# First group's inverse in blocks of sixteen joined by TensorE, single PSUM banks by name, and value transposes ahead of the state product

## The chip, the cores and the metric

One core of one Trainium2 chip runs the kernel. The metric is the device time of one execution in microseconds. Engines are TensorE (PE in the rows, with PEld for its weight loads), VectorE (DVE), ScalarE (ACT), GpSimd (POOL) and SyncE (SP), which issues most of the DMAs.

## The reference

A recurrent attention with a 40 x 40 state per head runs over 768 steps for 4 x 8 heads. Its output goes through a mixture of eight experts with a capacity, and then through a dense layer pair. Only the first part is touched by the change:

```
for t in range(S):
    y[:, :, t] = einsum('bhd,bhde->bhe', rt, state)
    Sa = einsum('bhde,bhe->bhd', state, at)
    state = state * wt[:, :, None, :] - einsum('bhd,bhe->bhde', Sa, bt) + einsum('bhd,bhe->bhde', vt, kt)
x = moe(y); out = relu(x @ w_in)**2 @ w_out
```

## The kernel before

**Chunks.** The 768 steps are cut into 24 chunks of 32 (`C`, `NC`). Within a chunk the recurrence is a triangular system: for each of the 32 heads a 32 x 32 strictly triangular matrix has to be inverted. One chunk fills eight columns of `GM`, `TT` and so on for four partition groups of 32, which makes 32 heads. Four chunks are a group, and one inverse serves a group.

**The inverse.** `inv_start` transposes `GM` to `L` (L228) and makes a list of jobs: seven small ones that build blocks of eight, two stages that double eight to sixteen, and two stages that double sixteen to thirty-two. A job is a product into a buffer `pr` and a sum over its last axis. `inv_all` (products L311, sums L314) does the first group's 27 jobs in one go before chunk 0; later groups are done by `inv` (L279, L283), so many jobs at a time, at places set by the tables `EARLY`, `FIRST`, `PLAN` and `LAST`. `inv_end` transposes the result to `TT` (L318), from which `block_T` copies block diagonals `TB` (L327).

**One chunk.** `scan` and `scale` (L158 to L189) turn the loaded tile `e` and `wB` into scaled factors. `gram` (L203) multiplies them to `G`, and `gram_mask` takes the two halves of `G` out of PSUM: ScalarE writes `GM`, VectorE writes `N`. `nat_n`, `nat_a`, `nat_pc` and `nat_k` lay out transposed copies. `solve` (px, L399) multiplies with `TB`, and ScalarE copies px to `lu`. `u` (pu) gives the new values, which ScalarE copies to `vu`. `state` (ps, L432) updates the state, `state_decay` writes it to `ru`, and `state_t` (pn) transposes it. `vu_t` (pv) transposes the values, ScalarE copies them to `vut`, `scores` (pq, L485) multiplies, and `scores_mask` (L493) masks on VectorE into `rq`. `y` (py) makes the output, `gate_in` writes `xt`, and the gate follows: `xT` (gpt), `logits` (pl), `choose`, `count` (pc), `rank`. `warm` issues matmuls whose results nobody reads.

**Order.** The whole attention part is written under a manual schedule: each engine does its instructions in the order of the Python calls in `run`. Chunks 1 to 19 run through `chunk(c)`, with m = c % 4; chunks 0 and 20 to 22 through the loop below it, chunk 23 by hand at the end. The expert part follows.

**PSUM.** Eight banks. Six are three double tiles, which `big` hands out in turn to G, pa, pk, px, pu, ps, pn, pv and most of the warm matmuls; two are single, handed out by `small` in turn to pq, py, gpt, pl, pc and the rest. A tile that is taken again waits until the readers of the one before are done:

```
return self.ps2.tile([128, 2, 512], F32, tag=f"b{self.nb % 3}", name=nm)
return self.ps1.tile([128, 512], F32, tag=f"s{self.ns % 2}", name=nm)
```

An fp32 matmul shows as two records in the trace, so that 32 matmuls stand there as x64.

Of the kernel before, what the change touches and what calls it, by code (L numbers as in the profile page):

```python
# [35 lines left out]
class Attention:  # L36
# [8 lines left out]
    def __init__(self, tc, es, gate, zt, eb, E, VN, VR, R0, R1, x, ident):  # L45
# [44 lines left out]
        self.st, self.nb, self.ns = {}, 0, 0  # L90
# [115 lines left out]
    def gram_mask(self, c, last=False):  # L206
# [9 lines left out]
        if not last:  # L216
            self.nc.scalar.mul(gm, gv[:, :, :, 0], -1.0)
        V.tensor_tensor(nn, gv[:, :, :, 1], self.mN.unsqueeze(1).unsqueeze(1).to_broadcast(bc), ALU.mult)
        if last:
            self.nc.scalar.mul(gm, gv[:, :, :, 0], -1.0)  # L220
# [80 lines left out]
    def inv_all(self):  # L301

        gi, jobs, _, _ = self.iv
        V = self.nc.vector
# [10 lines left out]
        self.inv_end()  # L315

# [86 lines left out]

    def u(self, c):
        A, V, T = self.nc.scalar, self.nc.vector, self.nc.tensor
        lu, rU, vu = self.lu, self.ru[c % 2], self.vu[c % 2]
        pu = self.big(f"pu{c}")
        for q in range(8):
            o, qq = q // 2, q % 2
            for par in range(2):  # L410
                for pp in range(2):
                    g, p = 2 * qq + pp, 64 * pp + 32 * par
                    T.matmul(pu[p : p + 32, q // 4, 40 * (q % 4) : 40 * (q % 4) + 40],
                             lu[:, par, o, 32 * g : 32 * g + 32], rU[:, par, q, 1 - pp, 0:40], start=True, stop=True)
# [81 lines left out]
    def y(self, c):  # L496
# [4 lines left out]
        py = self.small(f"py{c}")  # L501
# [29 lines left out]
    def run(self, extra, weights):  # L531
        LA, SHIFT = 7, 20
        EARLY, FIRST, PLAN, LAST = 4, (11, 8, 6, 2), (7, 5, 3, 1), (6, 5, 5, 0)
# [23 lines left out]
        self.warm(W0, self.zt, 320, True)  # L557
        for c in range(4):
# [13 lines left out]
        self.scan(4)  # L572
        self.scale(4)
# [29 lines left out]
        def chunk(c):  # L603
# [11 lines left out]
            if not done:  # L615
# [3 lines left out]
                self.gram_mask(c + LA)  # L619
# [54 lines left out]
            if ahead:  # L674
# [4 lines left out]
                self.gram_mask(c + LA + 1, True)  # L679
# [14 lines left out]
        def warm0(i):  # L694
            if c == 0:
                self.warm(W2[i], self.zt, 320, True)

        for c in range(NC - 1):
# [14 lines left out]
            if c == 0:  # L713
                self.gram(5)
# [23 lines left out]
            if c == 0:  # L738
                warm0(2)
# [101 lines left out]
class Gate:  # L841
# [44 lines left out]
    def xT(self, c):  # L886
# [4 lines left out]
        pt = self.at.small(f"gpt{c}")  # L891
# [8 lines left out]
    def logits(self, c):  # L900
# [4 lines left out]
        pl = self.at.small(f"pl{c}")  # L905
# [35 lines left out]
    def count(self, c0, c1):  # L941
# [3 lines left out]
        pc = self.at.small(f"pc{c0}")  # L945
# [796 lines left out]
```

## Time and profile before

| | us |
|---|---|
| median of 3 runs | 1092.46 (1089.16 to 1092.53) |
| profiled execution | 1095.65 |
| its span | 1093.9 |
| first px (chunk 0) starts | 69.66 |
| px of chunk 1 starts | 90.86 |
| attention part ends, about | 472 |

The span is what the trace covers; the execution's own time is 1.75 us longer. Times in the rows count from the span's start. Chunks are told apart by their matmuls: u(c) starts at 154.76 for c = 4, 221.95 for c = 8, 289.15 for c = 12, 351.45 for c = 16 and 402.41 for c = 20.

### The profile page before, as it was taken

To read this page: it belongs to the slowest core of one execution; us is meant where nothing else is said; L and a number is where in the kernel's file an instruction comes from. 1 tells how busy PE (TensorE), PEld (TensorE's weight loads), DVE (VectorE), ACT (ScalarE), POOL (GpSimd) and SP (SyncE) were. 2 spreads that over 40 slices of the span, in tenths; PEclk is the share of its full clock that TensorE was granted. 3 is DMA by queue.
4 is the path that set the end of the run, shared out by engine and by line. 5 is a ranking of instruction groups with operands and counts; after the bars stand their busy time and mean duration, and the time that the engine had idled before them with its cause. 6 is when DMAs were issued, how large, how long until landed. Compare 5 with 4: busy or idle time off the path is not lost.

```text
span 1093.9 us, 30647 instructions
## 1 busy us (share of the span) xinstructions
PE 932.5 (85%) x12526; PEld 838.5 (77%) x12526; DVE 744.2 (68%) x1486; ACT 585.8 (54%) x1330; POOL 313.8 (29%) x443
## 2 busy tenths in 40 slices
PE   4337788778787878898989998899999999999995
PEld 2236677667676767778979998789889899999995
DVE  5889989797899774558878878957544444444432
ACT  8125666676767877435545555456444353434332
POOL 4533225253354301115545555314301010000000
PEclk7668877896989998899989999899999999999998
DMA  7645634635453333165676766523100000000000
GB/s 183 148 134 149 210 92 146 182 111 166 141 150 94 98 110 110 43 179 163 210 227 204 217 216 200 163 85 105 49 25 25 25 25 25 1 25 1 25 1 28
DMA packets 80647, 122.71 MB, mean 112 GB/s; under 512 B 9679, under 2 KB 57409, under 8 KB 79561
## 3 DMA queue, kind: packets, MB, share of 16 engines
q1 hardware_dynamic: 71173, 100.09, 31.0%
q10 hardware_dynamic: 7020, 12.78, 4.1%
q0 software_dynamic: 2304, 7.78, 2.2%
q8 instruction: 101, 1.65, 0.6%
q14 instruction: 49, 0.40, 0.1%
HBM read 91.36 MB, written 29.35 MB: 110 GB/s over the span
## 4 chain that ended last, share of the span: by engine, by line
PE 56%; DVE 20%; ACT 10%; issue 5%; DMA 4%; POOL 3%; SPq 1%; ACTq 0%; DVEq 0%; POOLq 0%
PE phg L1405 16%; PE pog L1431 5%; PE pog L1430 5%; PE pog L1429 5%; PE phe L1405 4%; PE px L399 4%; DVE pr L279 2%; DMA xs<-zs_s 2%; PE ps L432 2%; ACT TB L327 2%; PE pq L485 2%; DVE pr L311 1%; PE poe L1431 1%; PE poe L1429 1%; PE poe L1430 1%
## 5 line engine op out<-in xcount | busy, mean ns | idle before, releaser
L1415 DVE SCALAR_TENSOR_TENSOR sqg<-phg,rg 128x512 f32<-128x512 f32 x96 | 66.3, 691 | 119.0 <-ACT rg L1414 116.8
L1414 ACT ACTIVATE rg<-phg 128x512 f32<-128x512 f32 x96 | 57.2, 596 | 110.4 <-PE phg L1405 110.2
L1417 DVE TENSOR_TENSOR hlg<-sqg,hhg 128x512 fp32r<-128x512 f32 x96 | 66.6, 694 | 65.9 <-ACT hhg L1416 61.1
L1416 ACT CAST hhg<-sqg 128x512 fp32r<-128x512 f32 x96 | 59.6, 620 | 78.6 <-DVE sqg L1415 76.2
L399 PE MATMUL px<-TB,X 128*104 128x128 f32 x384 | 66.1, 344 | 33.9 <-ACT TB L327 33.7
L1405 PE MATMUL phg<-xhg,e 128*128 128x512 f32 x264 | 93.1, 393 | 0.0
L399 PEld LDWEIGHTS px<-TB,X 128*104 128x104 f32 x384 | 60.5, 226 | 36.5 <-ACT TB L327 34.9
L1431 PE MATMUL pog<-e,hlg 128*128 128x320 f32 x240 | 74.2, 309 | 0.0
L1430 PE MATMUL pog<-e,hhg 128*128 128x320 f32 x240 | 74.1, 309 | 0.0
L1429 PE MATMUL pog<-e,hhg 128*128 128x320 f32 x240 | 73.9, 308 | 0.0
L186 POOL TENSOR_TENSOR e<-e 104x512 f32<-104x512 f32 x21 | 27.5, 1309 | 149.2 <-DVE e L162 79.5
L186 POOL TENSOR_TENSOR e<-e,wB 104x512 f32<-104x512 f32 x42 | 56.2, 1356 | 33.4 <-DVE wB L158 30.3
L1223 POOL TENSOR_TENSOR e<-rw,e 128x256 fp32r<-128x256 f32 x51 | 43.2, 851 | 69.3 <-ACT e L1222 65.5
L1405 PE MATMUL phe<-xhe,e 128*128 128x480 f32 (+4 forms) x176 | 58.6, 373 | 0.0
L1405 PEld LDWEIGHTS phg<-xhg,e 128*128 128x128 f32 x264 | 49.6, 188 | 8.9
L1544 POOL DMA_INDIRECT x2g<-zs_s,idx x24 | 23.7, 989 | 113.5 <-ACT hhg L1416 105.7
L327 ACT COPY TB<-TT 32x256 f32<-32x256 f32 x94 | 37.8, 402 | 34.5 <-DVE TT L318 28.4
L485 PE MATMUL pq<-rq,vut 128*64 128x64 f32 x768 | 39.2, 246 | 18.4 <-ACT vut L476 16.8
L203 PE MATMUL G<-e 64*32 64x64 f32 (+1 forms) x1536 | 24.0, 248 | 36.2 <-POOL e L186 23.1
L1431 PE MATMUL poe<-e,hle 128*120 128x320 f32 (+4 forms) x150 | 47.3, 315 | 7.2 <-DVE hle L1410 7.2
L203 PEld LDWEIGHTS G<-e 40*32 40x32 f32 (+1 forms) x1536 | 18.7, 117 | 43.6 <-POOL e L186 30.8
L1405 PE MATMUL phg<-xlg,e 128*128 128x512 f32 x132 | 51.8, 392 | 0.0
(340 smaller groups left out, 2920.5 us busy)
## 6 DMA issues: line engine op xcount, KB each, us to landing
e<-in_E_dram ACTq DMA_DIRECT2D x60, 208.0 KB
rw<-in_w_dram SPq DMA_DIRECT2D x30, 320.0 KB
zs_s<-zt SPq DMA_DIRECT2D x24, 320.0 KB
rw<-in_w_dram SPq DMA_DIRECT2D x30, 256.0 KB
e<-in_E_dram SPq DMA_DIRECT2D x9, 832.0 KB
ru<-in_VR_dram SPq DMA_DIRECT2D x48, 128.0 KB
cr<-in_wi_dram SPq DMA_DIRECT2D x20, 256.0 KB
cr<-in_wo_dram SPq DMA_DIRECT2D x20, 256.0 KB
```

Of the source, the lines that this page charges most:

```text
L186: eng.tensor_tensor(z, z, f, ALU.mult)
L327: (copies[g] if copies else self.nc.scalar.copy)(self.TB[c % 2][t, :, t], self.TT[t, 8 * (c % 4) : 8 * (c % 4) + 8])
L399: self.nc.tensor.matmul(px[0:104, par, 128 * o : 128 * o + 128], X[:, par, o, :], TB[:, 4 * par + o, :], start=True, stop=True)
L485: T.matmul(pq[s, 64 * q : 64 * q + 64], vut[:, q, s], rt[:, :, q, pp], start=True, stop=True)
L1405: T.matmul(o, lt, rt, start=(i == 0), stop=(i == len(seq) - 1))
L1414: A.activation(r[:, :n], o, AF.Relu)
L1415: V.scalar_tensor_tensor(sq[:, :n], o, 0.0, r[:, :n], ALU.max, ALU.mult)
L1416: A.copy(hh[:, :n], sq[:, :n])
L1417: V.tensor_tensor(hl[:, :n], sq[:, :n], b32(hh)[:, :n], ALU.subtract)
L1429: T.matmul(o, hh[:, t], W["h2"], start=(f == 0), stop=False)
L1430: T.matmul(o, hh[:, t], W["l2"], start=False, stop=False)
L1431: T.matmul(o, hl[:, t], W["h2"], start=False, stop=(f == NF - 1))
```

## The change

Five things, all within the attention part.

1. `inv_all` becomes `inv_blocks`: the first group's inverse stops at blocks of sixteen. A second, half transpose makes `nat`, and `join(c)` fills the missing sixteen-wide block of a chunk by two sets of 32 small matmuls (jl and jr) with a ScalarE copy between them and four copies behind. `join(0)` stands before the first `block_T`, `join(1)` behind `solve(0)`, `join(2)` and `join(3)` in chunk 0.
2. In the first four chunks and in `ahead`, VectorE's half of `gram_mask` comes before ScalarE's. `scan(4)` and `scale(4)` stand ahead of the first inverse's start, `scan(5)` ahead of `join(0)`.
3. PSUM is two double tiles in turn (G, pa, pk, ps, pn) and four single banks by name: 0 for pu and jl, 1 for px's and pv's first half and pq, 2 for py, gpt, pl, jr and the counts' pc of the first batches, 3 for the second halves of px and pv, for warm and for the later pc.
4. In `chunk`, `vu_t` stands ahead of `state`, and `state_decay` right behind it, on VectorE where m is 0 instead of on ScalarE. `scores` does one half of the partitions first, then the other. `nat_a` stands ahead of the gate's `xT`.
5. `EARLY` goes from 4 to 1, and the tables give those three jobs back: `PLAN` (8, 5, 4, 2), `LAST` (8, 6, 5, 0).

```diff
     def big(self, nm):
         self.nb += 1
-        return self.ps2.tile([128, 2, 512], F32, tag=f"b{self.nb % 3}", name=nm)
-
-    def small(self, nm):
-        self.ns += 1
-        return self.ps1.tile([128, 512], F32, tag=f"s{self.ns % 2}", name=nm)
+        return self.ps2.tile([128, 2, 512], F32, tag=f"b{self.nb % 2}", name=nm)
+
+    def bank(self, k, nm):
+        return self.ps1.tile([128, 512], F32, tag=f"k{k}", name=nm)
...
-    def inv_all(self):
+    def inv_blocks(self):
 
         gi, jobs, _, _ = self.iv
+        jobs = [j for j in jobs if j[0] < 9]
...
         self.inv_end()
+        nat = self.p2.tile([128, 512], F32, tag="prod", name="nat", bufs=3)
+        self.nat = nat.rearrange("p (a s) -> p a s", s=16)
+        V.transpose(self.nat.rearrange("p a s -> p s a"), self.Tt[:, 0:16])
+
+    def join(self, c, copies=None):
+
+        A, T = self.nc.scalar, self.nc.tensor
+        blocks = range(8 * c, 8 * c + 8)
+        groups = [slice(32 * g, 32 * g + 32) for g in range(4)]
+        p1, p2 = self.bank(0, f"jl{c}"), self.bank(2, f"jr{c}")
+        m = self.p2.tile([128, 512], F32, tag="prod", name=f"jm{c}", bufs=3)[:, 0:128]
+        for k, a in enumerate(blocks):
+            for s in groups:
+                T.matmul(p1[s, 16 * k : 16 * k + 16], self.GM[s, a], self.TT[s, a, 16:32], start=True, stop=True)
+        A.copy(m, p1[:, 0:128])
+        for k, a in enumerate(blocks):
+            for s in groups:
+                T.matmul(p2[s.start : s.start + 16, 16 * k : 16 * k + 16], self.nat[s, a], m[s, 16 * k : 16 * k + 16],
+                         start=True, stop=True)
+        for g, s in enumerate(groups):
+            h = slice(s.start, s.start + 16)
+            (copies[g] if copies else A.copy)(self.TT[h, 8 * c : 8 * c + 8, 16:32],
+                                              p2[h, 0:128].rearrange("p (a t) -> p a t", t=16))
...
-        px = self.big(f"px{c}")
+        px = [self.bank((1, 3)[par], f"px{par}_{c}") for par in range(2)]
...
-        pu = self.big(f"pu{c}")
+        pu = self.bank(0, f"pu{c}")
...
-        pv = self.big(f"pv{c}")
...
+        pv = [self.bank((1, 3)[pp], f"pv{pp}_{c}") for pp in range(2)]
...
-        pq = self.small(f"pq{c}")
-        for q in range(8):
-            for pp in range(2):
+        pq = self.bank(1, f"pq{c}")
+        for pp in range(2):
+            for q in range(8):
...
-        EARLY, FIRST, PLAN, LAST = 4, (11, 8, 6, 2), (7, 5, 3, 1), (6, 5, 5, 0)
+        EARLY, FIRST, PLAN, LAST = 1, (11, 8, 6, 2), (8, 5, 4, 2), (8, 6, 5, 0)
...
-        self.gram_mask(3, True)
+        self.scan(4)
+        self.gram_mask(3)
+        self.scale(4)
         self.inv_start(0, lambda k, h: G if (h, k) in POOL else V)
...
-        self.inv_all()
+        self.inv_blocks()
         self.load(8)
         A = self.nc.scalar
-        self.block_T(0, (A.copy, V.tensor_copy, A.copy, V.tensor_copy))
+        split = (A.copy, V.tensor_copy, A.copy, V.tensor_copy)
         self.scan(5)
+        self.join(0, split)
+        self.block_T(0, split)
         self.scale(5, (V, G, V))
         self.load_w(8)
         self.warm(W3)
         self.solve(0)
+        self.join(1)
...
             fill(c, 0)
+            self.vu_t(c)
             self.state(c)
-            if c % 2:
-                self.state_decay(c)
+            self.state_decay(c, None if c % 2 else V.tensor_copy if done else self.nc.scalar.copy)
             self.load(c + LA + 2, 3)
-            self.vu_t(c)
-            if c % 2 == 0:
-                self.state_decay(c, self.nc.scalar.copy)
...
+            self.nat_a(c + 2)
+            self.nat_n(c + 2)
+            self.nat_pc(c + 2)
             gate.xT(c - 1)
...
-            self.nat_n(c + 2)
-            self.nat_a(c + 2)
-            self.nat_pc(c + 2)
...
             if c == 0:
+                self.join(2)
                 self.gram(5)
...
             if c == 0:
+                self.join(3)
                 warm0(2)
...
-        pc = self.at.small(f"pc{c0}")
+        pc = self.at.bank(2 if c0 < 14 else 3, f"pc{c0}")
```

TensorE's order from the last Gram product before chunk 0 to the first ones in it. Before:

```order
L203 MATMUL G_480<-e_139 32x64 x32
L399 MATMUL px_612<-TB_108,X_104 104x128 x8
L413 MATMUL pu_636<-ru_110,lu 32x40 x32
L355 MATMUL pk_673<-ident_59,e_129 128x104 x8
L529 MATMUL warm<-zt 128x320
L203 MATMUL G_690<-e_362 32x64 x32
L432 MATMUL ps_730<-vu_112,rhsY_118 40x40 x32
```

And in the changed kernel at the same place:

```order
L202 MATMUL G_480<-e_139 32x64 x32
L329 MATMUL jl_568<-TT,GM 32x16 x32
L333 MATMUL jr_569<-jm_570,nat 16x16 x32
L422 MATMUL px_0_650<-TB_108,X_104 104x128 x4
L422 MATMUL px_0_651<-TB_108,X_104 104x128 x4
L329 MATMUL jl_662<-TT,GM 32x16 x32
L333 MATMUL jr_663<-jm_664,nat 16x16 x32
L436 MATMUL pu_747<-ru_110,lu 32x40 x32
L378 MATMUL pk_784<-ident_59,e_129 128x104 x8
L550 MATMUL warm<-zt 128x320
L329 MATMUL jl_801<-TT,GM 32x16 x32
L333 MATMUL jr_802<-jm_803,nat 16x16 x32
```

Two joins now stand between the first px and the next Gram product, and pu comes behind one of them.

TensorE's order in chunk 1, from the state product on. Before:

```order
L432 MATMUL ps_1126<-vu_113,rhsY_119 40x40 x32
L473 MATMUL pv_1163<-ident_59,vu_113 80x64 x16
L485 MATMUL pq_1197<-rq_117,vut 64x64 x16
L894 MATMUL gpt_1226<-ident_59,xt_1187 128x128 x2
L894 MATMUL gpt_1226<-ident_59,xt_1187 64x128
L355 MATMUL pa_1235<-ident_59,e_137 128x104 x8
L459 MATMUL pn_1248<-ident_59,ru_110 128x40 x16
```

In the changed kernel, from the last two value transposes on:

```order
L494 MATMUL pv_1_1384<-ident_59,vu_113 80x64
L494 MATMUL pv_1_1385<-ident_59,vu_113 80x64
L454 MATMUL ps_1404<-vu_113,rhsY_119 40x40 x32
L506 MATMUL pq_1456<-rq_117,vut 64x64 x16
L378 MATMUL pa_1485<-ident_59,e_137 128x104 x8
L917 MATMUL gpt_1500<-ident_59,xt_1446 128x128 x2
L917 MATMUL gpt_1500<-ident_59,xt_1446 64x128
L481 MATMUL pn_1507<-ident_59,ru_110 128x40 x16
```

ps has moved between pv and pq, and pa ahead of gpt.

TensorE's order in chunk 20 from the scores on, with the semaphores that each waits for. Before:

```order
L485 MATMUL pq_7147<-rq_116,vut 64x64 [waits DMAHW3_49,DMAHW1_49,Activation_49]
L485 MATMUL pq_7147<-rq_116,vut 64x64 [waits Activation_49]
L485 MATMUL pq_7147<-rq_116,vut 64x64 x14
L399 MATMUL px_7166<-TB_109,X_105 104x128 [waits PE_49]
L399 MATMUL px_7166<-TB_109,X_105 104x128 x7
L948 MATMUL pc_7183<-oh,mats 128x16 [waits PE_49,Activation_49]
```

In the changed kernel:

```order
L506 MATMUL pq_7443<-rq_116,vut 64x64 [waits Activation_49]
L506 MATMUL pq_7443<-rq_116,vut 64x64 x7
L422 MATMUL px_21_7462<-TB_109,X_105 104x128 [waits DVE_49,PE_49]
L422 MATMUL px_21_7462<-TB_109,X_105 104x128 x3
L422 MATMUL px_21_7463<-TB_109,X_105 104x128 x4
L971 MATMUL pc_7480<-oh,mats 128x16 [waits Activation_49]
```

px has a wait for VectorE that it did not have; the wait of pc for ScalarE now stands behind px's second half on the same bank.

## Rows read from the trace of the kernel before

**Rows 1.** The page, part 1: busy us, share of the span, instructions.

```profile
PE 932.5 (85%) x12526; PEld 838.5 (77%) x12526; DVE 744.2 (68%) x1486; ACT 585.8 (54%) x1330; POOL 313.8 (29%) x443
```

**Rows 2.** Stretches: length, busy us of PE, PEld, DVE, ACT, POOL, clock, DMA.

```profile
154.76:221.95 67.19, 54.53 (x1526) 49.01 (x1525) 56.89 (x102) 45.09 (x107) 24.81 (x41) 0.80 0.47 141
...
289.15:351.45 62.30, 48.50 (x1524) 42.78 (x1524) 56.88 (x101) 45.25 (x107) 29.85 (x48) 0.95 0.44 128
...
402.40:451.00 48.60, 40.30 (x1093) 36.16 (x1085) 22.66 (x64) 34.50 (x87) 4.61 (x5) 0.86 0.32 96
```

**Rows 3.** Timeline up to the inverse: start, us, instruction, idle before and releaser.

```profile
8.47 0.18 DVE L168 TENSOR_TENSOR Pc<-wB,e 104x16 f32<-104x16 f32 x1 [3.31 <-DMA e<-in_E_dram]
...
13.89 1.23 DVE L162 TENSOR_TENSOR_SCAN e<-e,ones 104x512 f32<-104x512 f32 x1 [2.42 <-DMA e<-in_E_dram]
...
22.83 0.42 DVE L218 TENSOR_TENSOR N<-G,mN 128x256 f32<-128x256 f32 x1 [4.55 <-ACT GM L217]
...
40.56 0.14 DVE L311 TENSOR_TENSOR pr<-L,Tt 128x4 f32<-128x4 f32 x1
40.72 1.26 POOL L186 TENSOR_TENSOR e<-e 104x512 f32<-104x512 f32 x1 [6.85 <-DVE pr L311]
...
46.84 0.63 DVE L311 TENSOR_TENSOR pr<-L,Tt 128x256 f32<-128x256 f32 x2
```

**Rows 4.** Timeline at the end of the first inverse.

```profile
51.79 2.10 DVE L311 TENSOR_TENSOR pr<-L,Tt 128x512 f32<-128x512 f32 x2
...
66.75 2.01 DVE L318 STREAM_TRANSPOSE TT<-Tt 128x1024 f32<-128x1024 f32 x1
...
69.66 3.46 PE L399 MATMUL px<-TB,X 128*104 128x128 f32 x16 [24.02 <-ACT TB L327]
...
71.20 1.23 DVE L158 TENSOR_TENSOR_SCAN wB<-wB,seeds 104x512 f32<-104x512 f32 x1
```

**Rows 5.** Timeline of the second group's inverse, first and eighth product.

```profile
95.13 0.24 DVE L279 TENSOR_TENSOR pr<-L,Tt 128x4 f32<-128x4 f32 x1
...
99.06 0.43 DVE L279 TENSOR_TENSOR pr<-L,Tt 128x256 f32<-128x256 f32 x1
```

**Rows 6.** Timeline of TensorE in chunk 0, to the px of chunk 1.

```profile
75.06 0.80 PE L413 MATMUL pu<-ru,lu 128*32 128x40 f32 x64 [1.94 <-DVE N L218]
...
83.22 0.85 PE L203 MATMUL G<-e 64*32 64x64 f32 x64 [1.82 <-DVE e L186]
...
89.75 1.18 PE L203 MATMUL G<-e 64*32 64x64 f32 x64 [3.25 <-DVE Pc L168]
...
90.86 3.11 PE L399 MATMUL px<-TB,X 128*104 128x128 f32 x16
```

**Rows 7.** Timeline of chunk 5 (first row) and of chunk 12.

```profile
180.93 0.90 PE L894 MATMUL gpt<-ident,xt 128*128 128x128 f32 x3 [0.97 <-DVE xt L516]
...
292.26 1.43 PE L432 MATMUL ps<-vu,rhsY 128*40 128x40 f32 x64
...
292.91 0.59 ACT L402 COPY lu<-px 104x512 f32<-104x512 f32 x1
...
294.97 0.33 PE L485 MATMUL pq<-rq,vut 128*64 128x64 f32 x2 [0.70 <-ACT vut L476]
...
301.67 0.62 PE L910 MATMUL pl<-wg,gxT 128*32 128x8 f32 x24 [3.27 <-ACT rhsY L463]
```

**Rows 8.** Timeline of chunks 19 and 20.

```profile
400.05 1.38 DVE L493 TENSOR_TENSOR rq<-pq,mQ 64x512 f32<-64x512 f32 x2
...
402.41 0.80 PE L413 MATMUL pu<-ru,lu 128*32 128x40 f32 x64
...
412.17 2.89 PE L399 MATMUL px<-TB,X 128*104 128x128 f32 x16
412.29 1.39 DVE L493 TENSOR_TENSOR rq<-pq,mQ 64x512 f32<-64x512 f32 x2 [3.03 <-PE pq L485]
...
415.15 1.07 ACT L402 COPY lu<-px 104x512 f32<-104x512 f32 x2 [3.24 <-PE px L399]
```

More of the change, by code (lines that the diff above doesn't have):

```diff
@@ L204, in gram, with gram_mask @@
                              e[r, 512 + 64 * i : 576 + 64 * i], start=True, stop=True)
-    def gram_mask(self, c, last=False):
+    def gram_mask(self, c, first=True):
         if c >= NC:
@@ L215, in gram_mask @@
         bc = [128, 2, 4, 32]
-        if not last:
+        if not first:
             self.nc.scalar.mul(gm, gv[:, :, :, 0], -1.0)
         V.tensor_tensor(nn, gv[:, :, :, 1], self.mN.unsqueeze(1).unsqueeze(1).to_broadcast(bc), ALU.mult)
-        if last:
+        if first:
             self.nc.scalar.mul(gm, gv[:, :, :, 0], -1.0)
@@ L412, in u @@
                     g, p = 2 * qq + pp, 64 * pp + 32 * par
[L413 removed]
+                    T.matmul(pu[p : p + 32, 40 * q : 40 * q + 40],
                              lu[:, par, o, 32 * g : 32 * g + 32], rU[:, par, q, 1 - pp, 0:40], start=True, stop=True)
@@ L467, in vu_t @@
         vu = self.vu[c % 2]
-        pv = self.big(f"pv{c}")
-        for h in range(2):
-            for i in range(4):
-                for pp in range(2):
-                    s = slice(64 * pp, 64 * pp + 64)
-                    T.transpose(pv[0:80, pp, 256 * h + 64 * i : 256 * h + 64 * i + 64],
-                                vu[s, pp, 4 * h + i].rearrange("p r d -> p (r d)"), self.ident[s, s])
+        pv = [self.bank((1, 3)[pp], f"pv{pp}_{c}") for pp in range(2)]
+        for q in range(8):
+            for pp in range(2):
+                s = slice(64 * pp, 64 * pp + 64)
+                T.transpose(pv[pp][0:80, 64 * q : 64 * q + 64], vu[s, pp, q].rearrange("p r d -> p (r d)"),
+                            self.ident[s, s])
         for pp in range(2):
-            A.copy(self.vut[0:80, :, 64 * pp : 64 * pp + 64], pv[0:80, pp].rearrange("p (q z) -> p q z", q=8))
+            A.copy(self.vut[0:80, :, 64 * pp : 64 * pp + 64], pv[pp][0:80].rearrange("p (q z) -> p q z", q=8))
     def scores(self, c):
@@ L480, in scores @@
         rt, vut = self.RT(c), self.vut
-        pq = self.small(f"pq{c}")
-        for q in range(8):
-            for pp in range(2):
+        pq = self.bank(1, f"pq{c}")
+        for pp in range(2):
+            for q in range(8):
                 s = slice(64 * pp, 64 * pp + 64)
@@ L500, in y @@
         lY, rY, pn = self.lhsY(c), self.rhsY[c % 2], self.st.pop(("Pn", c))
-        py = self.small(f"py{c}")
+        py = self.bank(2, f"py{c}")
         for o in range(4):
@@ L522, in store_x, with warm @@
         self.nc.sync.dma_start(self.x.rearrange("(b c t) f -> c b t f", b=4, c=NC)[c], self.gate.xt[c])
-    def warm(self, n, r=None, cols=512, small=False):
-        w = self.small("warm").unsqueeze(1).to_broadcast([128, 2, 512]) if small else self.big("warm")
+    def warm(self, n, r=None, cols=512):
+        w = self.bank(3, "warm").unsqueeze(1).to_broadcast([128, 2, 512])
         r = self.Tt.rearrange("p a b -> p (a b)") if r is None else r
@@ L556, in run @@
         G.memset(self.Tt.rearrange("p a b -> p (a b)")[:, 0:1024:33], 1.0)
-        self.warm(W0, self.zt, 320, True)
+        self.warm(W0, self.zt, 320)
         for c in range(4):
@@ L571, in run @@
         self.load_r(0)
-        self.scan(4)
-        self.scale(4)
         gate.init()
@@ L695, in warm0 @@
             if c == 0:
-                self.warm(W2[i], self.zt, 320, True)
+                self.warm(W2[i], self.zt, 320)
         for c in range(NC - 1):
@@ L890, in xT @@
         xt = self.xt[c]
-        pt = self.at.small(f"gpt{c}")
+        pt = self.at.bank(2, f"gpt{c}")
         for k in range(3):
@@ L904, in logits @@
         xT = self.xTt.pop(c)
-        pl = self.at.small(f"pl{c}")
+        pl = self.at.bank(2, f"pl{c}")
         for k in range(3):
```

15 lines of the change are left out of this document (7 added, 8 removed).

## The prediction

> **What bounds the kernel now.** I read the page first, then the stretches, then the timeline of the places that the diff touches. TensorE is busy 85% of the span and VectorE 68% [rows 1], but that is a mean over stages. The diff ends with the attention part; the expert part after it keeps its instructions, so whatever the attention part gains or loses in its last microsecond is passed on whole. Within the attention part there are four stages. Up to the first px at 69.66 VectorE runs alone, and its inverse is the chain. In chunk 0, from px at 69.66 to px at 90.86, TensorE waits three times for what VectorE delivers [rows 4, 6]. In chunks 1 to 18 the two take turns: a stretch of four chunks takes 67.2 or 62.3 us with VectorE busy 56.9 in both [rows 2]. From chunk 19 VectorE has less to do and TensorE's order decides.
>
> **First stage.** Four steps move the first px.
> - VectorE's first N waits 4.55 us for ScalarE, which reads the same G [rows 3]. With the order turned, it can run at 18.28. Loads hold it next: VectorE got the first two E at 8.47 and 13.89, 5.4 apart, so the third is there at 19.3, the fourth at 24.7, the fifth with its wB near 30. Then a scan pair (two scans of 1.23 [rows 4] with the small steps between them, 3.0), N and GM (0.42 each, as N's row) and a transpose (2.0) lead to the first product at 36.5 instead of 40.56: -4.0. Bounds -1.5 (loads later) and -4.55.
> - The seven small products took 40.56 to 46.84, 6.28 us, beside GpSimd's multiplications of scale(4), which begin at 40.72 [rows 3]; the same seven took 3.93 in the second group [rows 5]. Scale(4), three pieces of 1.26, can now start at 33.4, before N and the transpose, and ends at 37.2, just after the first product begins: one slowed product is left. I take -1.5, bounds 0 and -2.35. [...]
> - The sixteen-wide stage, from 51.8 to the transpose at 66.75, goes: -14.9 [rows 4].
> - Between the transpose's end and px stood 0.9 us. Now nat's transpose (half of 2.01: 1.0), the scan pair of chunk 5 (3.0) and TT's copies on VectorE (0.55) stand there, with the join of TensorE and ScalarE beside them: 32 matmuls, a copy, 32 matmuls, a copy, 3.0 if 32 matmuls cost 1.2, as G's do [rows 6]. Net +4.4; bounds +3 and +6.
>
> The first px: 69.66 - 4.0 - 1.5 - 14.9 + 4.4 = 53.7, 16.0 earlier.
>
> **Chunk 0.** It held 21.2 us from px to px. Three more joins stand in TensorE's order, each 32 + 32 matmuls with a ScalarE copy between (0.3, half of lu's 0.59 for four times the columns [rows 7]): 2.7, together +8.1 (at 0.80 for 32, as pu's [rows 6], +5.7). ScalarE reaches the copies of joins 2 and 3 late, behind four TB copies and two ru copies: +3.8 (0 to 5). The px of chunk 1 now takes a bank that scores(0) filled, and its mask stands behind scan(8) in VectorE's order: +2.0. Against that the three waits fall away, 1.94, 1.82 and 3.25 [rows 6], since VectorE comes 16 us earlier: -7.0. Sum +6.9, so the next px comes at 81.7, not 90.86: **-9.2** of the 16.0 stay. Bounds -13 and -6.
>
> **Chunks 1 to 18**, for each four:
> - In the first of the four, pl waits 3.27 for a bank that the mask frees late [rows 7]; on its own bank it doesn't. Two products with sums fewer stand before the mask and the gate's input; at 1.05 for a product [rows 4] and 0.4 for a sum (a pass over 256 columns takes 0.43 [rows 5]) that is, with smaller shapes among them, some -2.4. VectorE takes ru's two copies from ScalarE there: +1.6 (a 64x512 pair is 1.39 [rows 8]). VectorE being the chain at this place, -0.8.
> - pa goes ahead of gpt, which waited 0.97 for VectorE [rows 7]: -0.9.
> - The transposes of the values stand ahead of the state product, so the 1.43 us of ps cover ScalarE's copy for which pq waited 0.70 [rows 7]. In two chunks of four I count all of it, in the third half (ps must wait for pk's copies, with two double buffers instead of three), in the first nothing: there pv takes px's banks and must wait until lu is copied, 293.50, where ps could start at 292.26 [rows 7]. -1.75.
> - One more product and sum stands between the last mask and the transpose: +1.45.
>
> That is -2.0 for four chunks, **-9.0** over 4.5. Bounds: 0 where VectorE eats it, and -21 where all stretches fall to VectorE's own 56.9 + 1.6 [rows 2].
>
> **Chunks 19 to 23.** Here the new banks cost. px lies on banks 1 and 3, pq on bank 1, the gate's counts on bank 3.
> - Chunk 19: px was done before the mask (400.05 to 401.43) began, and pu followed at 402.41 [rows 8]. Now px waits for the mask's end: 2.9 for px and 0.7 of the transposes behind it, +3.6.
> - Chunk 20: px started at 412.17 with the mask at 412.29; now after it, +1.5. The counts then wait for lu's copies, which end at 416.22 where px ended at 415.06 [rows 8]: +1.2. With a slower px, +3.3.
> - Chunk 21 +1.5 (mask alone); chunk 22 +2.6 (mask, and the warm matmul on bank 3 behind lu); chunk 23 +1.7 (counts behind vut's copies, two of the same size as lu's 1.07).
>
> Sum **+12.7**; behind these matmuls stand y, pa, pl and the next u, for which all wait. Bounds +7 (lu's first half copied while px's second half runs) and +18 (a lower clock on top). For the other terms, cost is nothing: nat on VectorE beside the join (1.0 if not), GM after N on an idle ScalarE.
>
> **Sum:** -9.2 - 9.0 + 12.7 = -5.5. The profiled execution took 1095.65 us (span 1093.9), 3.2 over the median of 1092.46; the difference is put on the median: 1087.0.
>
> **The rivals.**
> - *The start is kept*: joins 2 and 3 hide under VectorE and ScalarE comes in time, -13 instead of -9.2, and the tail costs its lower bound 7: -15, 1077.5. For it: TensorE idles 7.0 us in chunk 0 [rows 6]. Against: the join's copies stand in ScalarE's order behind others. 0.17.
> - *The clock rises in the middle*: the stretch from 154.76 had a granted clock of 0.80 and kept TensorE busy 54.5 us; that from 289.15 had 0.95 and 48.5 for as many instructions, and took 4.9 us less [rows 2]. If fewer waits bring two stretches there, -10 more: 1077. 0.10.
> - *The clock falls in the tail*: the waits added from chunk 19 leave TensorE idle, and its clock goes to the lower level more often. At the price that separates the two stretches, 6.0 of busy time, the tail is +18.7: 1093, no change. 0.08. [...]
> - *VectorE eats the middle*: two fewer early products come back as the late one, no gain in chunks 1 to 18: +3.5, 1096. For it: VectorE is 85 to 91% busy there. 0.17.
> - *Slower*: pv, moved ahead of ps, stalls on lu's copies not in one chunk of four but in every chunk that solves ahead. Place: between px and pv; price 1.24 [rows 7] in the ten others, +12.4: 1099. It decides from 0.9 us per chunk on, where the gain of 5.5 has become a loss of 3.3. Against: in the others y, pk and G stand between. 0.12.
>
> **How the numbers follow.** The forecast has 0.36 and its own range 1082 to 1092. The range takes in 1077 and leaves out the slower rival and what lies beyond the bounds: 1075 to 1098. About 0.3%, 3.3 us, is what a measurement here can tell from no change, so faster is below 1089.2. Faster: 0.28 of the forecast, 0.17, 0.10 and 0.02 make 0.57. Slower: 0.12, and 0.10 of the middle eaten, 0.22. The rest, 0.21, is no change.
>
> **What would show it.** First px near 53.7, the second near 81.7; no N waiting for ScalarE before the first inverse. Scores starting without a wait for vut in chunks 1 to 18, ps directly ahead of them. In chunks 19 to 22 px beginning at the mask's end, and pc or warm behind lu. I am wrong if px(0) is earlier by 16 and px(1) by as much, if the stretches of four shrink by over 5 us, or if the last chunks take no longer than the 48.6 us that they did from 402.40 to 451 [rows 2].

## The result, and the profile after

The changed kernel takes 1104.5 us (four executions, 1103.2 to 1107.4), the kernel before 1092.5 beside it: 1.0113 times as long, interval 1.0076 to 1.0151. Six more executions gave 1103.9 (1.0122, 1.0078 to 1.0166). The forecast was 1087.0 and its range ended at 1098, so it is wrong in sign and outside the range. The kernel before scatters by itself: 35 executions lay between 1081.3 and 1103.2, with a median of 1091.7.

The table shows where the time went, in the profiled execution of each kernel (1107.4 and 1095.65 us). u(c) is the start of pu of chunk c on TensorE, and pte is the first matmul of the expert part:

| | before | after | difference |
|---|---|---|---|
| first px | 69.66 | 54.05 | -15.6 |
| px of chunk 1 | 90.86 | 83.35 | -7.5 |
| u(1) | 94.71 | 85.96 | -8.7 |
| u(8) | 221.95 | 211.00 | -11.0 |
| u(16) | 351.45 | 341.56 | -9.9 |
| u(19) | 388.06 | 375.32 | -12.7 |
| u(20) | 402.41 | 397.88 | -4.5 |
| u(21) | 417.80 | 419.44 | +1.6 |
| u(22) | 433.22 | 434.85 | +1.6 |
| u(23) | 450.39 | 455.02 | +4.6 |
| first pte of the expert part | 469.11 | 475.80 | +6.7 |
| end of the span | 1093.9 | 1105.7 | +11.8 |

Up to chunk 19 the kernel is ahead by 12.7 us. Chunks 19 to 23 lose 19.4, and the expert part another 5.1, which a second profile below shows to be scatter. The page's first part says nothing of this; VectorE has even less to do than in [rows 1]:

```profile
PE 952.9 (86%) x13038; PEld 857.6 (78%) x13038; DVE 733.2 (66%) x1477; ACT 586.3 (53%) x1340; POOL 305.3 (28%) x439
```

The stretches are four chunks, u(12) to u(16), and then chunks 19 to 23 whole (from u(19) to the first pte). Columns as in [rows 2]: length, busy us of PE, PEld, DVE, ACT, POOL, granted clock, DMA share, GB/s.

```profile
277.26:341.56 64.30, 53.36 (x1525) 47.37 (x1524) 59.97 (x106) 44.43 (x106) 31.05 (x48) 0.87 0.43 124
375.32:475.80 100.48, 73.14 (x1614) 63.82 (x1607) 48.68 (x165) 50.01 (x127) 10.96 (x12) 0.81 0.25 73
```

The four chunks from 277.26 took 64.30, with VectorE busy for 59.97 of it; the same four took 62.30 in [rows 2]. Chunks 19 to 23 took 100.48 us for TensorE's 73.14 busy ones. The same chunks in the kernel before:

```profile
388.06:469.11 81.05, 67.64 (x1622) 58.99 (x1615) 47.23 (x166) 48.90 (x127) 10.74 (x12) 0.86 0.30 88
```

So of the 19.4 lost, 5.5 are slower matmuls (about as many of them, at a granted clock of 0.81 instead of 0.86) and 13.9 are idle time. A second profile of the changed kernel has 102.3 us for the same chunks.

VectorE's timeline (start, duration, idle before and its releaser in brackets) shows that the first stage went as planned:

```profile
17.91 0.41 DVE L217 TENSOR_TENSOR N<-G,mN 128x256 f32<-128x256 f32 x1
...
36.83 0.92 DVE L311 TENSOR_TENSOR pr<-L,Tt 128x4 f32<-128x4 f32 x1
...
41.43 1.15 DVE L311 TENSOR_TENSOR pr<-L,Tt 128x256 f32<-128x256 f32 x2
...
46.42 2.01 DVE L341 STREAM_TRANSPOSE TT<-Tt 128x1024 f32<-128x1024 f32 x1
48.24 1.08 DVE L318 STREAM_TRANSPOSE nat<-Tt 128x512 f32<-128x512 f32 x1
```

N at 17.91 no longer waits for ScalarE, where it waited 4.55 [rows 3]; the first product is at 36.83 (36.5 was forecast), and the seven small ones are done at 41.43, after 4.60 instead of 6.28. No sixteen-wide stage follows; the transpose does at 46.42. TensorE in chunk 0:

```profile
54.05 3.71 PE L422 MATMUL px<-TB,X 128*104 128x128 f32 x16 [3.41 <-DVE TB L350]
...
66.45 0.72 PE L333 MATMUL jr<-jm,nat 32*16 32x16 f32 x64 [2.37 <-ACT jm L330]
...
74.31 0.69 PE L333 MATMUL jr<-jm,nat 32*16 32x16 f32 x64 [2.05 <-ACT jm L330]
...
83.35 1.97 PE L422 MATMUL px<-TB,X 128*104 128x128 f32 x16 [0.75 <-DVE rq L514]
```

Joins 2 and 3 wait 2.37 and 2.05 for ScalarE's copy, and the second px 0.75 for the mask.

TensorE from 90 to 374 us, which is all but the ends of chunks 1 to 18, grouped by line: busy us and mean ns, then the idle time ahead of the group and what ended it.

```profile
L506 PE MATMUL pq<-rq,vut 128*64 128x64 f32 x576 | 36.2, 229 | 4.8 <-issue 4.1 <-ACT vut L497 0.7
L454 PE MATMUL ps<-vu,rhsY 128*40 128x40 f32 x1152 | 28.0, 216 | 2.2 <-ACT rhsY L411 2.2
...
L378 PE MATMUL pa<-ident,e 104*128 104x104 f32 x144 | 16.8, 260 | 6.3 <-DVE N L217 6.3
...
L528 PE MATMUL py<-rhsY,rq 128*32 128x40 f32 x1152 | 16.3, 218 | 4.5 <-ACT lg L934 4.5
...
L494 PE MATMUL pv<-ident,vu 64*80 64x64 f32 x288 | 13.4, 230 | 2.7 <-ACT lu L425 2.7
...
L917 PE MATMUL gpt<-ident,xt 128*128 128x128 f32 (+1 forms) x54 | 10.2, 302 | 5.7 <-DVE xt L537 5.7
L933 PE MATMUL pl<-wg,gxT 128*32 128x8 f32 (+1 forms) x408 | 8.8, 188 | 10.6 <-ACT gxT L920 10.6
```

Before, over its own chunks 1 to 18 (94.71 to 388.06), pq idled 16.8 us, 15.8 of it for vut:

```profile
L485 PE MATMUL pq<-rq,vut 128*64 128x64 f32 x576 | 30.2, 244 | 16.8 <-ACT vut L476 15.8 <-issue 1.1
```

There pl idled 8.0, py 0.9, ps 0.7, pa nothing, and pv did not wait for lu. In the changed kernel the wait for vut is down to 0.7, as meant. In its place pl waits 10.6 for gxT, pa 6.3 for N, py 4.5 for lg, pv 2.7 for lu, ps 2.2.

TensorE in chunks 19 and 20:

```profile
380.57 1.90 PE L506 MATMUL pq<-rq,vut 128*64 128x64 f32 x32 [0.34 <-ACT vut L497]
390.53 3.71 PE L422 MATMUL px<-TB,X 128*104 128x128 f32 x16 [8.06 <-DVE rq L514]
394.03 1.59 PE L378 MATMUL pa<-ident,e 104*128 104x104 f32 x8
395.42 0.71 PE L917 MATMUL gpt<-ident,xt 128*128 128x128 f32 x3
396.06 0.69 PE L481 MATMUL pn<-ident,ru 40*128 40x40 f32 x16
397.46 0.49 PE L933 MATMUL pl<-wg,gxT 128*32 128x8 f32 x24 [0.72 <-ACT gxT L920]
397.88 0.80 PE L436 MATMUL pu<-ru,lu 128*32 128x40 f32 x64
...
409.92 3.42 PE L422 MATMUL px<-TB,X 128*104 128x128 f32 x16 [1.58 <-DVE rq L514]
414.07 1.06 PE L971 MATMUL pc<-oh,mats 128*128 128x16 f32 x8 [0.73 <-ACT lu L425]
...
419.02 0.49 PE L933 MATMUL pl<-wg,gxT 128*32 128x8 f32 x24 [2.29 <-DVE xt L537]
```

and ScalarE and VectorE at the first of these waits:

```profile
383.29 1.64 ACT L350 COPY TB<-TT 32x256 f32<-32x256 f32 x4 [2.29 <-DVE ab L980]
...
386.90 1.66 DVE L469 TENSOR_TENSOR ru<-ps,Pc 40x640 f32<-40x640 f32 x2
...
389.00 1.38 DVE L514 TENSOR_TENSOR rq<-pq,mQ 64x512 f32<-64x512 f32 x2
```

px of chunk 20 idles 8.06 us until the mask is done, although TB, its last input, was there at 384.93. The scores that the mask reads had ended at 382.47, but VectorE did the gate's ranks, ru and xt first and came to the mask at 389.00. px then takes 3.71 us, where the same px took 1.99 before,

```profile
396.33 1.99 PE L399 MATMUL px<-TB,X 128*104 128x128 f32 x16 [0.52 <-ACT TB L327]
```

and all that follows (pa, gpt, pn, pl) stands behind it: from the mask's end at 390.38 to pu at 397.88 are 7.5 us, where [rows 8] had 1.0.

### The profile page after: what moved, and what is told of

Its sections match the earlier page's. It is cut to its first block, busy times and chain, and to the rows that moved or that the text cites. A ratio compares the mean times of both kernels' runs of the same rounds, so it can differ in the third digit from the quotient of the medians.

```text
span 1105.7 us, 31651 instructions
## 1 busy us (share of the span) xinstructions
PE 952.9 (86%) x13038; PEld 857.6 (78%) x13038; DVE 733.2 (66%) x1477; ACT 586.3 (53%) x1340; POOL 305.3 (28%) x439
## 4 chain that ended last, share of the span: by engine, by line
PE 54%; DVE 23%; DMA 8%; ACT 7%; issue 5%; SPq 1%; POOL 1%; ACTq 0%; DVEq 0%; POOLq 0%
PE phg L1428 16%; PE pog L1454 5%; PE pog L1453 5%; PE pog L1452 5%; DVE pr L278 5%; PE phe L1428 4%; PE px L422 3%; PE pq L506 2%; DMA xs<-zs_s 2%; DVE rq L514 2%; DVE Tt L282 2%; DMA wB<-in_E_dram 2%; DVE e L161 1%; DMA rw<-in_w_dram 1%; PE ps L454 1%
## 5 line engine op out<-in xcount | busy, mean ns | idle before, releaser
L185 POOL TENSOR_TENSOR e<-e,wB 104x512 f32<-104x512 f32 x42 | 55.4, 1335 | 35.1 <-DVE wB L157 26.4
L506 PE MATMUL pq<-rq,vut 128*64 128x64 f32 x768 | 52.6, 242 | 5.7 <-issue 4.1
L506 PEld LDWEIGHTS pq<-rq,vut 128*64 128x64 f32 x768 | 49.1, 154 | 7.7 <-issue 5.4
L1432 ACT ACTIVATE hhe<-phe 128x480 fp32r<-128x480 f32 (+4 forms) x64 | 33.9, 529 | 33.2 <-PE phe L1428 33.0
L514 DVE TENSOR_TENSOR rq<-pq,mQ 64x512 f32<-64x512 f32 x48 | 32.9, 685 | 21.9 <-PE pq L506 21.2
```

Source lines behind the costliest of these rows:

```text
L185: eng.tensor_tensor(z, z, f, ALU.mult)
L506: T.matmul(pq[s, 64 * q : 64 * q + 64], vut[:, q, s], rt[:, :, q, pp], start=True, stop=True)
```

## Experiments

For chunks 19 to 23 there are three theories. A: the shared single banks lengthen them. B: the moved orders make VectorE or ScalarE late. C: TensorE's clock is lower. For the middle: either the new banks take back what the moves earn, or VectorE is the chain and nothing done to TensorE's waits counts. Times are medians of 6 to 12 executions of the experiment and 17 to 35 of the kernel before beside them.

**Scores off px's bank, in the last chunks.**

```diff
-        pq = self.bank(1, f"pq{c}")
+        pq = self.bank(0 if c >= 19 else 1, f"pq{c}")
```

> The changed kernel, but from chunk 19 on scores writes to bank 0 (pu's, read long before) instead of px's bank 1, so that px no longer stands behind the mask. Theory A, that the shared banks lengthen the last chunks: px of chunk 20 starts near 385.5, when TB is there, instead of 390.53, and the three waits of 1.57 ahead of the later px go; 6.5 for chunk 19 and 1.6 for each of chunks 20 to 22 make -11, 1093, with the first pte near 464.5 instead of 475.80. Rival B, that the last chunks are longer because the moved orders make VectorE or ScalarE late: px waits for something else, less than 3 us come back, 1102 to 1105. Rival C, a lower clock of TensorE: the waits go but matmuls stay slow, -5, 1099.

1091.3 us (1.0026 of before, 0.9988 to 1.0063): one bank number is worth 13 us. TensorE, and the stretch from u(19) to the first pte:

```profile
384.61 3.74 PE L422 MATMUL px<-TB,X 128*104 128x128 f32 x16 [2.58 <-ACT TB L350]
...
402.75 2.81 PE L422 MATMUL px<-TB,X 128*104 128x128 f32 x16
...
411.24 0.63 PE L933 MATMUL pl<-wg,gxT 128*32 128x8 f32 x24 [2.30 <-DVE xt L537]
```

```profile
374.89:463.20 88.31, 70.41 (x1614) 61.81 (x1607) 48.83 (x166) 50.08 (x127) 10.97 (x12) 0.86 0.29 83
```

px of chunk 20 starts at 384.61 behind TB and not behind the mask, that of chunk 21 without a wait; pl still waits 2.30 for xt. Idle time of the stretch fell from 27.3 to 17.9, busy time by 2.7, the clock rose from 0.81 to 0.86. Theory A holds; B falls, since the orders are still moved; C accounts for the busy part at most.

**All banks of the last chunks apart.** In addition:

```diff
-        px = [self.bank((1, 3)[par], f"px{par}_{c}") for par in range(2)]
+        if c >= 20:
+            pxb = self.big(f"px{c}")
+            px = [pxb[:, par] for par in range(2)]
+        else:
+            px = [self.bank((1, 3)[par], f"px{par}_{c}") for par in range(2)]
...
-        pt = self.at.bank(2, f"gpt{c}")
+        pt = self.at.bank(1 if c >= 18 else 2, f"gpt{c}")
...
-        pl = self.at.bank(2, f"pl{c}")
+        pl = self.at.bank(1 if c >= 18 else 2, f"pl{c}")
```

> As the run on the scores' bank, and in addition px from chunk 20 on a double tile, as before the change, and gpt and pl of the last chunks on bank 1 instead of py's bank 2; so the counts and warm no longer wait for lu, and pl no longer for the gate's input. Theory A: beyond -11 another 2.3 for pl in chunk 20, 0.7 for the counts there, 1.3 in chunk 22 and 1.1 in chunk 23, together -16, 1088, and the stretch of the last chunks as long as before the change. Rival B: as the run on the scores' bank or no gain, 1102 to 1105. Rival C: half of it, 1097.

1091.0 (1.0004, 0.9971 to 1.0036), no better than the run before it and 3 us above what was expected. TensorE shows why:

```profile
403.55 1.99 PE L426 MATMUL px<-TB,X 128*104 128x128 f32 x16
...
416.05 0.64 PE L498 MATMUL pv<-ident,vu 64*80 64x64 f32 x16 [2.47 <-ACT gxT L924]
...
432.35 1.07 PE L498 MATMUL pv<-ident,vu 64*80 64x64 f32 x16 [2.46 <-ACT gxT L924]
```

px of chunk 21 follows at once, but I had put gpt on pv's bank, and pv now waits 2.47 and 2.46 for ScalarE to copy gpt. The edit made the kind of wait that it was to remove.

**The last chunks mended.** px and scores as there, gpt left alone, and

```diff
-        pl = self.at.bank(2, f"pl{c}")
+        pl = self.at.bank(3 if c >= 19 else 2, f"pl{c}")
```

> The changed kernel with scores on bank 0 and px on a double tile from chunk 19 on, as in the run on the last chunks' banks, but gpt stays on bank 2 and only pl goes to bank 3; in that run gpt on bank 1 made the value transposes wait 2.47, 2.46 and 1.00 us for ScalarE's copy of gpt. Theory A: those 5.9 us come back, less what was gained elsewhere; 1086 to 1088, and from the pu of chunk 19 to the first pte some 80, against 85.5 there and 81.05 before the change. If the last chunks are slow for another reason: 1091 again.

1086.6 (0.9965, 0.9937 to 0.9994), 17 us below the changed kernel. From u(19) to the first pte:

```profile
372.82:455.11 82.29, 66.53 (x1615) 57.49 (x1608) 48.67 (x168) 49.26 (x127) 10.74 (x12) 0.92 0.31 91
```

82.29 against 81.05 before the change and 100.48 with it; idle 15.8, clock 0.92. The last chunks' banks explain the loss.

**The start alone.** The kernel before with `inv_blocks`, the joins (their tiles from `small`) and the order of `scan(4)`, `scale(4)` and the two halves of the mask; no named banks, no moves.

```diff
-        self.gram_mask(3, True)
+        self.scan(4)
+        self.gram_mask(3)
+        self.scale(4)
...
-        self.inv_all()
+        self.inv_blocks()
...
         self.scan(5)
+        self.join(0, split)
+        self.block_T(0, split)
```

> The kernel before, with the first stage alone changed: blocks of sixteen, nat, the four joins, the order of scan(4), scale(4) and of the two halves of the Gram mask; three double tiles and two turning singles stay. Theory A, with the start's gain passed on: px of chunk 0 near 54, that of chunk 1 near 83, and -7.5 to -8.7 in the end, 1084. If VectorE or a fixed wait later takes the gain back, 1089 to 1092; if the joins wait longer on the turning singles, px of chunk 1 near 86 and 1088.

1085.4 (0.9938, 0.9901 to 0.9975), 6.3 below the median of before beside it. px of chunk 0 at 53.65, of chunk 1 at 82.50. From u(19) on:

```profile
372.21:453.90 81.69, 68.24 (x1622) 59.48 (x1615) 47.55 (x167) 49.51 (x127) 9.76 (x11) 0.84 0.30 86
```

**The wait alone, in the start alone.**

```diff
-        pq = self.small(f"pq{c}")
+        if 19 <= c < 23:
+            pq = self.big(f"pq{c}")[:, 0]
+            self.nb -= 1
+            self.ns += 1
+        else:
+            pq = self.small(f"pq{c}")
```

> The start alone, with one cost added: from chunk 19 to 22 scores write to the first half of the double tile that px of the next chunk takes, so px must stand behind the mask, as in the changed kernel; all orders and other tiles as in the start alone. Theory A: what the run on the scores' bank gave back is lost here, +13 on 1085.4, bounds +8 (the sum by the trace) and +13: 1093 to 1098, with px of chunk 20 at the end of the mask. Rival B, that the loss needs the moved orders: +3 at most, 1088.

1094.4 (1.0025, 0.9993 to 1.0056): +9.1, with none of the moves. TensorE at px of chunks 20 and 21, then the stretch:

```profile
387.42 3.71 PE L423 MATMUL px<-TB,X 128*104 128x128 f32 x16 [6.02 <-DVE rq L522]
...
404.62 1.97 PE L423 MATMUL px<-TB,X 128*104 128x128 f32 x16 [1.59 <-DVE rq L522]
```

```profile
373.60:465.14 91.54, 67.93 (x1621) 59.65 (x1615) 49.88 (x186) 49.30 (x128) 9.75 (x11) 0.84 0.26 76
```

The stretch grew by 9.9 us against the start alone while busy time (67.93) and clock (0.84) stayed: here the wait is the whole price.

**The middle's moves undone**, in the changed kernel (start and banks stay).

```diff
-            self.vu_t(c)
             self.state(c)
...
+            self.vu_t(c)
...
-        EARLY, FIRST, PLAN, LAST = 1, (11, 8, 6, 2), (8, 5, 4, 2), (8, 6, 5, 0)
+        EARLY, FIRST, PLAN, LAST = 4, (11, 8, 6, 2), (7, 5, 3, 1), (6, 5, 5, 0)
```

> The changed kernel, with the middle's moves undone: state product ahead of the value transposes, state_decay as before the change, pa behind gpt, and the four tables of early jobs as before. Start and banks stay changed. If the moves earn what the trace shows from chunk 1 to 19 (4.0), the time rises by 4 to 1108.5; if they earn the predicted 9.0, to 1113.5; if the moves are to blame for the long wait of chunk 19 (theory B), it falls by 4 or more, to 1100 or below.

1102.7 (1.0083, 1.0049 to 1.0116): within what a measurement tells of the changed kernel's 1104. Its profile took 295.0 from u(1) to u(19), against 289.4, but it is of the longest of the twelve executions (1110.1). The start alone, which has none of the moves and keeps the old tiles, took less from u(1) to u(19) than the changed kernel:

```profile
85.17:372.21 287.04, 231.66 (x6736) 206.88 (x6735) 253.59 (x465) 202.49 (x480) 107.58 (x178) 0.86 0.49 143
```

```profile
85.96:375.32 289.36, 236.30 (x6736) 212.09 (x6735) 256.41 (x471) 197.47 (x471) 106.38 (x178) 0.87 0.49 140
```

The first row is the start alone, the second the changed kernel. TensorE's idle time is 55.4 us without the moves and 53.1 with them, so the waits changed places and hardly went away. The moves earned nothing that can be measured on the new banks.

**The start and the moves, on the old tiles.**

```diff
+            self.vu_t(c)
             self.state(c)
-            if c % 2:
-                self.state_decay(c)
+            self.state_decay(c, None if c % 2 else V.tensor_copy if done else self.nc.scalar.copy)
...
-            self.vu_t(c)
```

> The kernel before with the first stage changed (1085.4 by the run of the start alone) and the middle's moves too: value transposes ahead of the state product, state_decay behind it and on VectorE in each fourth chunk, scores one half of the partitions first, pa ahead of gpt, the four tables; three double tiles and two turning singles stay, so the new banks are the only part left out. Theory A, that the new banks take back what the moves earn: scores lose the 14.9 us for which they waited for vut in chunks 1 to 18, part of it comes through, 1078 (-4 to -9). Theory B, that VectorE is the chain there and eats it: 1085, no change to the start alone. Rival: two kinds of tile in turn put other waits behind the moved orders, 1089 or more.

1082.5 (0.9929, 0.9894 to 0.9965), the fastest of all, but the start alone had 0.9938, so a gain from the moves is not shown here either; from u(1) to u(19) this profile took 287.7, the start alone 287.0. Scores and pl in chunks 1 to 18:

```profile
L509 PE MATMUL pq<-rq,vut 128*64 128x64 f32 x576 | 36.4, 229 | 5.1 <-issue 4.6 <-ACT vut L500 0.4
...
L936 PE MATMUL pl<-wg,gxT 128*32 128x8 f32 (+1 forms) x432 | 8.9, 183 | 15.9 <-DVE rq L517 9.2 <-ACT gxT L922 6.7
```

Scores' wait for vut is gone here too (15.6 in the start alone), and pl's has grown from 8.6 to 15.9.

**py and pl apart in the middle as well,** and px from chunk 20 on a double tile.

```diff
-        pq = self.bank(1, f"pq{c}")
+        pq = self.bank(0, f"pq{c}")
...
-        pt = self.at.bank(2, f"gpt{c}")
+        pt = self.at.bank(1, f"gpt{c}")
...
-        pl = self.at.bank(2, f"pl{c}")
+        pl = self.at.bank(1, f"pl{c}")
```

> The changed kernel with scores on bank 0 in every chunk, px from chunk 20 on a double tile, and gpt and pl on bank 1 in every chunk, so that py no longer waits for ScalarE's copy of pl (4.5 us in chunks 1 to 18) nor pl for the gate's input. Theory A for the middle as well: 1091 less 4.5, and less part of pl's 9.9 behind gxT, 1085. If only the last chunks' banks matter: 1091, as the run on the last chunks' banks. The 8.0 us for which pa waits behind N for a double tile stay in either case.

1090.95 (1.0010, 0.9978 to 1.0043), not 1085.

```profile
L426 PE MATMUL px<-TB,X 128*104 128x128 f32 x280 | 51.9, 361 | 10.5 <-ACT TB L350 9.4 <-ACT lg L938 1.1
...
L532 PE MATMUL py<-rhsY,rq 128*32 128x40 f32 x1152 | 16.5, 216 | 1.8 <-issue 1.8
...
L937 PE MATMUL pl<-wg,gxT 128*32 128x8 f32 (+1 forms) x408 | 8.7, 186 | 11.4 <-ACT gxT L924 11.4
```

py's 4.5 fell to 1.8, and px's idle time rose to 10.5 (9.4 of it for TB) from 4.5 in the changed kernel over the same window. TB is copied from the end of the inverse on VectorE, so a wait removed on TensorE came back as a wait for what VectorE delivers.

**A little more of VectorE, a little more of TensorE,** in chunks 1 to 18 of the changed kernel.

```diff
+            if c < 19:
+                more = self.p2.tile([128, 512], F32, tag="prod1", name=f"more{c}", bufs=1)
+                V.tensor_tensor(more, self.ones[:, 0:512], self.ones[:, 0:512], ALU.mult)
             self.scan(c + LA + 2)
```

> The changed kernel with one more VectorE product of 128x512 (about 1.05 us, both inputs constant, result unread) at the end of each of chunks 1 to 18. If VectorE is the chain of the middle, which is why neither the moves nor the banks there change the time: +15 to +19, 1119 to 1123. If TensorE's waits and order set the time: +5 or less, 1109.

```diff
             self.scores(c)
+            if c < 19:
+                self.warm(1, idle, 512)
```

> The changed kernel with one more matmul of 512 columns (about 1.0 us at the upper clock, result unread, constant inputs, on bank 3) behind the scores of each of chunks 1 to 18. If VectorE is the chain of the middle: +5 or less, 1109, perhaps less still where the matmul lifts the granted clock. If TensorE sets the time: +18 or more, 1122.

The added instructions in the two profiles (x34 records are 17 matmuls):

```profile
L710 DVE TENSOR_TENSOR more<-ones 128x512 f32<-128x512 f32 x16 | 11.1, 692 | 0.6
```

```profile
L550 PE MATMUL warm<-mats 128*128 128x512 f32 x34 | 19.1, 645 | 0.0
```

VectorE's 18 products are 12.5 us, and the time became 1112.5 (1.0197, 1.0157 to 1.0236), 8.6 over 1103.9. From u(1) to u(19), where 17 of them lie (11.8 us), it rose by 11.0, from 289.4 to 300.4: nearly all that is added to VectorE came through there. VectorE's busy time in that stretch grew by 13.2, TensorE's by 2.9.

TensorE's 18 matmuls are 20.2 us, and the time became 1107.4 (1.0133, 1.0092 to 1.0174). That is 3.5 more, which is within the scatter. From u(1) to u(19) it rose by 4.0:

```profile
88.00:381.32 293.32, 239.47 (x6771) 205.80 (x6770) 258.71 (x464) 195.65 (x471) 108.34 (x178) 0.94 0.48 139
```

This run does not settle what it was made for. The granted clock rose from 0.87 to 0.94, the other matmuls became shorter, and TensorE's busy time grew only from 236.3 to 239.5. So 3.2 us were added in the end and 4.0 came through. That VectorE holds the middle rests on the run with more of VectorE and on the moves that earned nothing; that TensorE does not hold it as well is not shown. I had sized the added product at 1.05 us from the inverse's row; it took 0.69.

**The changed kernel again.**

> The changed kernel as it is, on the same chip as the three others, to have its time from more executions and a second profile of its expert part, which in the first took 629.9 us from the first pte to the end, where the kernel before took 624.8. If that is a scatter of executions, near 625 now; if the change lengthens it, near 630 again. The time: 1104.5.

1103.9. Its expert part took 625.7 us in this profile, not 629.9. All thirteen profiles, of before, after and the experiments, have 622.6 to 629.9, so the 5.1 us of the first table are scatter.

## Why the prediction was wrong

- **First stage, -16.0:** -15.6. The order of N and the loads gave -3.7 (predicted -4.0), the small products -1.7 (-1.5), and from the transpose's end to px 5.6 stood instead of 0.9, +4.7 (+4.4). Right, term by term. Beside GpSimd's scale(4), 33.98 to 37.73, the transpose took 2.13, as without it (2.10 before), and one product was slowed (the first, 0.92, where it took 0.24 in [rows 5]). That the -1.5 left one slowed product and a transpose at its old length was my estimate, which no row of the kernel before shows; this run does.
- **Chunk 0, +6.9:** +8.1. The waits of joins 2 and 3 are there (4.4 together against 3.8), px behind the mask is 0.75 instead of 2.0. A size slightly off. Alone, the start is worth 6.3 us at the end by the medians; the interval, 2.7 to 10.8, holds the predicted 9.2.
- **Chunks 1 to 18, -9.0: failed, and it is the larger miss.** I added up TensorE's waits as if each that goes were time gained. The wait for vut went (15.8 to 0.7), and others came (pl, pa, py, pv, ps). u(1) to u(19) shrank by 4.0 against the profile before, but the moves did not bring that: without them the start alone took 287.0, less than the changed kernel's 289.4, and undoing them cost nothing that can be measured. That the middle earns nothing is what I had as a rival at 0.17; that VectorE is what eats it is borne out by the 11.0 us that came through of 11.8 added to VectorE. Smaller steps were wrong too. The row of 2.10 us in [rows 4] is two products of different shapes, 0.68 and 1.51, so 1.05 is the price of neither; with `EARLY` at 1 instead of 4, three products and not two leave the place before the mask; and the bound of -21 does not follow from [rows 2], whose stretches of 67.2 and 62.3, brought down to 58.5, would give -28 on the mean.
- **Chunks 19 to 23, +12.7: failed by its size.** They measured +19.4 in the profile, and by medians 17.3 us came back when their banks were mended. The place and the mechanism were right: px at the mask's end, pc and warm behind lu. The waits also came near in sum, 13.9 us of idle time added. They lay elsewhere than I put them: chunk 19 lost 8.2 against 3.6, because not 0.7 but 3.6 lie between px's end and pu (2.5 of pa, gpt and pn, pl's own wait of 0.72 and 0.4 of pl), px took 3.71 and not 2.9, and u(19) came 12.7 earlier while the mask came only 11.05 earlier. In chunk 20 I missed that pl shares bank 2 with py and so waits 2.29 for the gate's input, behind the ranks in VectorE's order: 6.2 against 3.3. Chunk 21 lost nothing (+1.5), 22 and 23 were 3.0 and 2.1 (+2.6, +1.7). On top came 5.5 us of slower matmuls (granted clock 0.81 instead of 0.86), which I had as a separate rival (the clock falls in the tail, 6.0, 0.08). How much of that the waits brought about stays open: with scores off px's bank the stretch's clock was 0.86 again, but in the start alone the same wait cost 9.9 with the clock at 0.84 as without it. Waits and a low clock do lie together where px of chunk 20 stood in the changed kernel: TensorE idled from 382.47 to 390.53, and from 385.8 on its granted clock was 0.50. The slow px of chunk 20 is not the bank's doing alone: its granted clock was 0.50 in the changed kernel, where it took 3.71 (before 1.00 and 1.99), and with scores off its bank it took 3.74 as well, after a wait of 2.58 for TB.
- **Slower by pv behind lu:** 2.7 us in all of chunks 1 to 18, not 12.4. Refuted.
- **The expert part passes it on whole:** it did, within its own scatter of 7 us.

Put together by medians: -6.3 for the start alone (-9.2 forecast), nothing in the middle (-9.0) and +17.3 for the last chunks (+12.7) make +11.0, near the measured 12. Neither miss alone would have left the range: the middle at nothing gives 1096, the last chunks at +17.3 give 1091.6, and both 1100.6. I gave a chance to each rival alone and none to two at once, and my own bounds for the two terms, 0 and +18, taken together already give 1101.3, beyond the range's end of 1098. The middle's mistake in one sentence: removing a wait of TensorE earned nothing where TensorE's other waits took its place.

The runs speak against scores and px on one bank in the last chunks: it cost 13 us in the changed kernel (1104.5 against 1091.3) and 9.1 in the start alone (1094.4 against 1085.4), and with turning tiles none of it. What stays open is a difference of some 4 us between the mended kernel (1086.6) and start and moves on the old tiles (1082.5). Their intervals overlap, so it may be scatter; if not, pa's wait for N with only two double tiles is a candidate that was not tried alone.

## What to carry to other kernels

Give PSUM banks by the life of what lies in them: list for each bank who reads last, on which engine, and what is queued ahead of that reader; the next tile on the bank starts there, however early its inputs are (px of chunk 20 stood until the mask's end at 390.38, with its last input there at 384.93). Before costing waits, find the chain of each stage by adding a known piece of work to one engine, and read from the same stretch how much busy time was really added: on VectorE 11.0 of 11.8 us came through, while with 20.2 us of matmuls TensorE's granted clock was 0.94 instead of 0.87 and its busy time only 3.2 us longer, so that run told little. Keep the part of a change that stands alone: the start's part here makes a faster kernel (1085.4), and with the moves on the old tiles it has 1082.5, while the PSUM tiles of the change cost 21 us on top.

## What the runs showed of the hardware

With the added, unread matmuls the granted clock was higher: 0.94 instead of 0.87 from u(1) to u(19). The same four chunks as above, u(12) to u(16), with them:

```profile
278.99:342.59 63.60, 50.76 (x1532) 43.18 (x1532) 59.38 (x104) 43.22 (x105) 30.79 (x48) 1.00 0.44 125
```

The granted clock is 1.00, where the changed kernel had 0.87, and TensorE is busy 50.76 us instead of 53.36, with four matmuls of 1.1 us more. This is why 20.2 us of added matmuls made TensorE's busy time only 3.2 us longer.

A VectorE product of 128x512 took 0.692 us with plain inputs. In the same profile the inverse's products of that size, with sums left out, are these:

```profile
L278 DVE TENSOR_TENSOR pr<-Xm,Tt 128x512 f32<-128x512 f32 x8 | 8.4, 1052 | 0.3
...
L278 DVE TENSOR_TENSOR pr<-L,Tt 128x512 f32<-128x512 f32 x9 | 6.5, 724 | 0.3
```

The inputs of both kinds are views that repeat an axis (`left` and `right` in `inv_start`). Eight of the nine products of L took 0.69, as with plain inputs, and one 0.98, so the repeated axis is not what costs. The products of Xm took 1.03 to 1.09; their view of Tt steps by 32 elements along the last axis, where those of L step by one. The step alone was not tried.
